# Attention with agents and a one-expert mixture on one core: a first batch's instructions reordered, constant products added, and the last blocks' scaling moved between engines

## The chip, the cores and the metric

The kernel runs on one core of one Trainium2 chip. The metric is the device time of one execution in microseconds (us); the median of several executions is compared. The core's engines are TensorE (PE in the rows; PEld is its weight loading), VectorE (DVE), ScalarE (ACT), GpSimd (POOL) and SyncE (SP), which here issues nearly all DMA transfers. Each engine works through its own list of instructions in order, and waits in that order.

## The reference

Four batches of 11456 tokens with 128 channels pass through an attention with 49 "agents" in the middle; the result is the input of a mixture of 8 experts with one expert per token.

```python
scale = 1.0 / np.sqrt(128)                       # sm(a, b): softmax over rows of scale * a @ b.T
agent_v = sm(agents, k) @ v                      # (49 x 128) per batch: needs all keys and values
attn    = sm(q, agents) @ agent_v                # per token
x       = attn.reshape(B * S, 128)               # 45824 tokens
logits  = x @ w_gate;  e = argmax(logits);  p = softmax(logits)[e]
out     = p * (relu(x @ w1[e]) @ w2[e])          # 128 -> 1024 -> 128
```

## The kernel before

**Per batch.** A batch's tokens come in 12 chunks (11 of 1024 tokens, one of 192). Keys: each chunk is loaded (`ld`), its sum of squares gives a power of two as scale (`scale_bits`, lines 232 and 236 on VectorE, 239 on GpSimd), it is split into two half-precision parts (`split`: L403, then L406, or L417 and L418), turned by a transposing DMA (`hT`, L432) and multiplied with the agents (`scores`, L475 to L479). After the last key the maximum is formed (`keymax`), the exponentials taken (`kexp`, L557 and L562), and the values multiplied (`values`: in the first batch L595, in later ones L612, which needs the parts `eh` that GpSimd's L574 and L582 help to make). `agentvalues` and `choose` then find the expert that most tokens of the batch want (`ei`, L826, named `gate["D"]`), and its weights are loaded (L264, L266) and folded with the agents' values into `Ah`, `Al` (L845 to L852). Queries give `E` (L722 to L730) and the matrix `M`, turned by another transposing DMA (L753).

**Steps.** The chosen expert is then applied to the whole batch in 184 steps (23 groups of 512 tokens by 8 slices of the hidden layer): L1341 and L1342 multiply `M` with `Ah`, `Al`; L1344 (ScalarE) and L1345 (VectorE) make `hh`; L1359 multiplies with `w2h`, `w2l`. 736 steps in all. The next batch's attention runs beside them. Its events stand in a list by step numbers: `KS1` are those of the second batch's keys, `QC`, `Q0` those of the first batch's queries from the fourth on, at step `Q0 + 13 * (c - 3)`. A scheduler then orders each engine's list; `queued("D")` keeps instructions behind `gate["D"]` on that instruction's engine, VectorE, alone.

**Before the steps.** The first batch has nothing to run beside, so TensorE waits for single results. `busy(n, x)` issues n products of constants (L526, 512 columns each) behind the instruction x, whose result nobody reads.

**Rank sums.** When a batch's routing is known, `leftover_ranks` sums where tokens of other experts go (L988 to L1005, on GpSimd in the first three batches).

**Tail.** Tokens that chose another expert than their batch's are gathered in 14 blocks of 128. Per block the expert's w1 and w2 are loaded and split (`weights_split`: L1198 on ScalarE, L1200 on VectorE, or instead of L1200 a second pass of ScalarE and GpSimd's L1203); `block_layer1` has 24 matmuls (L1212 to L1214), L1216 and L1217; `block_layer2` has 24 more (L1228 to L1230); `block_store` scales the result (L1237, VectorE) and scatters it (L1243, issued by GpSimd). The loop over u runs layer 1 of block u, then layer 2 of block u - 2, then the weights of block u + 5.

Of the kernel before, what the change touches and what calls it, by code (L numbers as in the profile page):

```python
# [16 lines left out]
AF = mybir.ActivationFunctionType  # L17
ALU = mybir.AluOpType
# [4 lines left out]
A = 49  # L23
# [22 lines left out]
KS0, KT0, KL0, VT0, VL0, QS0, QL0 = -200, 2, 4, 2, 1, (-175, -142, -141.5), (2.8, 1.2, 1.3)  # L46
VE, T1, TF0, TF1, TL, TLM, Q0 = 12, 1.75, 3, 1.5, 18, 10, 5

# [3 lines left out]
QM0, QG0 = (-145.5, -140, 0), ("K", "D", ("A", 1))  # L52
KS1 = [-142, -141.5] + [8.2 * i for i in range(10)]
KS2 = {0: 7, 1: 11}
# [17 lines left out]
FL, FLS, FW, FWJ, WA, FS, SPA, FSE = 148, (0, 2, 12), 104, 10.5, 7, 8, 7, 'D'  # L72
TSE, BL = 'D', 2
AHEAD, AHEAD0 = 3, 8
# [4 lines left out]
def agent_moe_kernel(ctx, tc, q, k, v, agents, wg, w1, w2, out):  # L79
    nc = tc.nc  # L80
# [141 lines left out]
    def queued(x):  # L222
        return tc.issue_after(gate[x].ins) if x in gate else nullcontext()
# [67 lines left out]
    def attention(b):  # L291
# [94 lines left out]

        def scaling(src, c, ss, p):
            SC[src, c] = scale_bits(ss, p, 1, "s" + src, AG["bits"] if src != "v" else None)

# [79 lines left out]
        def scores(src, c, ps):  # L469
            _, p, t = chunks[c]  # L470
            x = TT.pop((src, c))
            for i in range(t):
                o = ps[:p, i * A:(i + 1) * A]
                if how[src, c] == "X":
                    nc.tensor.matmul(o, x[:, i, :p], AG["T"], start=True, stop=True)  # L475
                    continue
# [52 lines left out]
        def keymax(i):  # L529
# [12 lines left out]
            else:  # L542
                pt = small_ps()
                x = nc.tensor.matmul(pt[:, :A], ones[:A, :], MX["d"][:A], start=True, stop=True)
                if first:
                    busy(6, x)
                mxb = MX["b"] = one.tile([P, A], F32, tag="mxb", name="mxb")
# [75 lines left out]
        def agentvalues(i):  # L623
# [12 lines left out]
            elif i == 2:  # L636
# [4 lines left out]
                if first:  # L641
                    pt = small_ps()
                    nc.tensor.matmul(pt[:, :A], AV["acc"][:, :D], both, start=True, stop=True)
                    AV["acc"] = pt[:, :A]
# [547 lines left out]
    def weights_split(u, j, eng):  # L1192
# [4 lines left out]
            [P, 2, FF], F16, tag=tag, name="wsp", **({} if tag == "ld" else dict(bufs=HLB if tag == "hl" else HTB[tag[2:]])))  # L1197
        nc.scalar.activation(hl[:, 0, :], x, AF.Copy, scale=m)  # L1198
        if eng == "D":
            nc.vector.scalar_tensor_tensor(hl[:, 1, :], x, m, hl[:, 0, :], op0=ALU.mult, op1=ALU.subtract)  # L1200
        else:
            nc.scalar.activation(x, x, AF.Copy, scale=m)
            nc.gpsimd.tensor_tensor(hl[:, 1, :], x, hl[:, 0, :], op=ALU.subtract)  # L1203
# [28 lines left out]
    def block_store(u):  # L1232
# [3 lines left out]
        yo = xg[1][:, u % 4, :]  # L1236
        nc.vector.tensor_scalar(yo, bh.pop(u)[:, :D], gt, None, op0=ALU.mult)  # L1237
        view = oviews[u]
# [286 lines left out]
```

## Time and profile before

| | us |
|---|---|
| median of 3 runs (lowest to highest) | 1103.39 (1100.06 to 1105.75) |
| the profiled execution, its own time | 1102.89 |
| its span, first to last instruction | 1101.2 |
| TensorE busy | 1021.1 (93%) |
| VectorE busy | 982.1 (89%) |
| ScalarE busy | 828.6 (75%) |
| GpSimd busy | 213.2 (19%) |

The profile is of one execution. The span leaves out 1.7 us that lie around it. A busy TensorE is not one at its peak, since it runs at one of two clocks, 1.2 or 2.4 GHz; the profile gives the granted clock as 0.5 or 1.0. Idle time counts only where the engine that waits is one that sets the pace.

### The profile page before, as it was taken

The page shows a single profiled execution, that of the slowest core. Times are in us where ns is not written, and L with a number is a line of the kernel's source. Part 1 is how long each engine was busy: PE and PEld are TensorE (multiplying, and loading weights), DVE is VectorE, ACT ScalarE, POOL GpSimd, SP SyncE. Part 2 cuts the span into 40 slices and gives each one's busy share as a digit, 9 for nine tenths or more (in the row PEclk, how much of TensorE's full clock was granted, in tenths as well). Part 3 has the DMA queues.
Part 4 walks back from the last instruction along what each step waited for, and adds up shares of the span by engine and source line. Part 5 has one row for each costly group of instructions (what it writes and reads, how often), then busy time and mean ns, then how long its engine had stood idle before and what let it go on. Part 6 is the DMA issues. An engine that isn't in the chain of part 4 may idle for free. (4 is left out here: it accounts for less than half of the span.)

```text
span 1101.2 us, 35748 instructions
## 1 busy us (share of the span) xinstructions
PE 1021.1 (93%) x14590; PEld 824.8 (75%) x14590; DVE 982.1 (89%) x2350; ACT 828.6 (75%) x1495; POOL 213.2 (19%) x373
## 2 busy tenths in 40 slices
PE   7979989999889999999999999999999999989995
PEld 7757767777667777777787777777777777767895
DVE  5659989998789999998999998998999999899894
ACT  6558767888678787889888887988677666667591
POOL 1020001233500011133400011232400223111043
PEclk9968999999899999999999999999999999999998
DMA  9779979544289899765399998563466556434460
GB/s 322 213 189 229 206 166 211 147 128 149 96 174 239 187 236 195 200 138 189 116 227 228 212 231 210 136 186 133 119 170 139 151 120 122 143 110 131 152 216 15
DMA packets 269384, 189.44 MB, mean 172 GB/s; under 512 B 211273, under 2 KB 235426, under 8 KB 269216
## 3 DMA queue, kind: packets, MB, share of 16 engines
q1 hardware_dynamic: 267648, 184.87, 66.6%
q0 software_dynamic: 1568, 2.25, 1.1%
q8 instruction: 115, 1.88, 0.7%
q14 instruction: 53, 0.43, 0.1%
HBM read 99.75 MB, written 36.43 MB: 124 GB/s over the span
## 5 line engine op out<-in xcount | busy, mean ns | idle before, releaser
L1359 PEld LDWEIGHTS <-hh 128*128 128x128 f16 x8640 | 547.6, 99 | 170.2 <-issue 7.4
L1359 PE MATMUL py<-w2h,hh 128*128 128x128 f16 (+1 forms) x5760 | 606.5, 220 | 2.7 <-ACT hh L1344 1.4
L1359 PE MATMUL py<-w2l,hh 128*128 128x128 f16 (+1 forms) x2880 | 523.8, 220 | 1.7 <-DVE w2l L899 1.7
L1344 ACT ACTIVATE hh<-ph 128x512 f16<-128x512 f32 (+1 forms) x736 | 412.9, 583 | 133.4 <-PE ph L1342 125.4
L1345 DVE SCALAR_TENSOR_TENSOR hh<-ph,hh 128x512 f16<-128x512 f32 (+1 forms) x736 | 476.8, 666 | 31.9 <-ACT hh L1344 30.6
L1341 PE MATMUL ph<-M,Ah 128*128 128x512 f16 (+1 forms) x736 | 276.1, 376 | 22.5 <-DVE hh L1345 21.4
L1342 PE MATMUL ph<-M,Al 128*128 128x512 f16 (+1 forms) x736 | 276.2, 375 | 0.0
L406 DVE SCALAR_TENSOR_TENSOR hl<-ld,mul,hl 128x1024 f16<-128x1024 f32 (+1 forms) x115 | 139.9, 1220 | 18.3 <-ACT hl L403 16.9
L403 ACT ACTIVATE hl<-ld,mul 128x1024 f16<-128x1024 f32 (+1 forms) x117 | 127.0, 1092 | 24.2 <-DVE mul L236 23.5
L369 ACT ACTIVATE jk<-ld 128x1024 f16<-128x1024 f32 (+1 forms) x124 | 124.3, 1003 | 10.5 <-DMA ld<-in_k_dram 10.3
L239 POOL TENSOR_SCALAR div<-hb,bits 128x1 int32<-128x1 int32 (+1 forms) x88 | 28.6, 325 | 430.2 <-DVE hb L232 407.5
L1342 PEld LDWEIGHTS <-Al 128*128 128x128 f16 x736 | 72.1, 98 | 31.2 <-issue 29.1
L1341 PEld LDWEIGHTS <-Ah 128*128 128x128 f16 x736 | 73.5, 100 | 4.8 <-issue 3.1
L1372 DVE TENSOR_TENSOR yo<-py,cs 128x512 f32<-128x512 f32 (+1 forms) x92 | 61.4, 668 | 1.0 <-PE py L1359 0.9
L477 PE MATMUL ps_s<-agh,hT 128*128 128x49 f16 x580 | 52.9, 185 | 3.6 <-DMA hT<-hl 2.1
L479 PE MATMUL ps_s<-agh,hT 128*128 128x49 f16 x580 | 52.8, 184 | 0.0
L478 PE MATMUL ps_s<-agl,hT 128*128 128x49 f16 x580 | 52.7, 184 | 0.0
L574 POOL TENSOR_TENSOR es<-es,S 128x392 f32<-128x392 f32 (+1 forms) x33 | 32.1, 973 | 102.7 <-ACT S L562 96.4
L477 PEld LDWEIGHTS <-hT 128*128 128x128 f16 x606 | 49.5, 97 | 3.2 <-DMA hT<-hl 3.2
L478 PEld LDWEIGHTS <-hT 128*128 128x128 f16 x606 | 48.3, 97 | 2.3 <-issue 2.0
L479 PEld LDWEIGHTS <-hT 128*128 128x128 f16 x606 | 48.2, 97 | 0.1
L562 ACT ACTIVATE S<-S,ln 128x392 f32<-128x392 f32 (+1 forms) x48 | 27.7, 598 | 17.4 <-DVE S L557 17.3
(323 smaller groups left out, 1349.1 us busy)
## 6 DMA issues: line engine op xcount, KB each, us to landing
ld<-in_k_dram SPq DMA_DIRECT2D x44, 512.0 KB
ld<-in_v_dram SPq DMA_DIRECT2D x44, 512.0 KB
ld<-in_q_dram SPq DMA_DIRECT2D x44, 512.0 KB
out_dram<-yo SPq DMA_DIRECT2D x88, 256.0 KB
w1e<-in_moe_w_dram SPq DMA_DIRECT2D x18, 512.0 KB
w2e<-in_moe_w_dram SPq DMA_DIRECT2D x18, 512.0 KB
exps<-E SPq DMA_DIRECT2D x44, 196.0 KB
wn<-in_moe_w_dram SPq DMA_DIRECT2D x16, 512.0 KB
```

The costliest lines, as they stand in the source:

```text
L369: nc.scalar.activation(jk[:p, :t * D], x[:p, :t, :].rearrange("p t d -> p (t d)"), AF.Square, accum_out=ss[:p])
L403: nc.scalar.activation(hi[:p, :t, :], x[:p, :t, :], AF.Copy, scale=m)
L406: nc.vector.scalar_tensor_tensor(lo[:p, :t, :], x[:p, :t, :], m, hi[:p, :t, :], op0=ALU.mult, op1=ALU.subtract)
L477: nc.tensor.matmul(o, x[:, 0, i, :p], AG["h"], start=True, stop=False)
L478: nc.tensor.matmul(o, x[:, 0, i, :p], AG["l"], start=False, stop=False)
L479: nc.tensor.matmul(o, x[:, 1, i, :p], AG["h"], start=False, stop=True)
L1341: x1 = nc.tensor.matmul(ph[:, :nn], st['Ah'][:, f, :], m, start=True, stop=False)
L1342: nc.tensor.matmul(ph[:, :nn], st['Al'][:, f, :], m, start=False, stop=True)
L1344: x2 = nc.scalar.activation(hh[:, 0, :nn], ph[:, :nn], AF.Relu)
L1345: x3 = nc.vector.scalar_tensor_tensor(hh[:, 1, :nn], ph[:, :nn], 0.0, hh[:, 0, :nn], op0=ALU.max, op1=ALU.subtract)
L1359: mm_ = lambda l, r, **k: nc.tensor.matmul(o, l, r, skip_group_check=True, **k)
L1372: nc.vector.tensor_tensor(yo[:p, :n, :], py[:p, :n * D].rearrange("p (i d) -> p i d", d=D), cs.unsqueeze(2).broadcast_to([p, n, D]), op=AL ...
```

## The change

Six edits:

1. The scale bits of the second batch's first two keys (`KS2` holds chunks 0 and 1) are made under `queued("D")`: VectorE's L232 and L236 for them stand behind the expert's choice. Their events move from step -142 and -141.5 to -141.9 and -141.4.
2. Constant products: four after the scores of the first batch's first query chunk, four after the product of `agentvalues(2)` in the first batch, and four in place of six after `keymax(2)`.
3. `Q0` goes from 5 to 1: every event of the first batch's queries from the fourth chunk on is four steps earlier, loads, transposes and `M` too.
4. `TSE` goes from `'D'` to `'DDDP'`: of the 14 splits of the tail's loop, those of w2 for three blocks (8, 10 and 12) go by ScalarE and GpSimd.
5. That path is rewritten: GpSimd scales the weights in place, ScalarE rounds, GpSimd subtracts.
6. `block_store` scales on ScalarE.

```diff
-VE, T1, TF0, TF1, TL, TLM, Q0 = 12, 1.75, 3, 1.5, 18, 10, 5
+VE, T1, TF0, TF1, TL, TLM, Q0 = 12, 1.75, 3, 1.5, 18, 10, 1
-KS1 = [-142, -141.5] + [8.2 * i for i in range(10)]
+KS1 = [-141.9, -141.4] + [8.2 * i for i in range(10)]
-TSE, BL = 'D', 2
+TSE, BL = 'DDDP', 2
         def scaling(src, c, ss, p):
+            with queued("D") if b == 1 and src == "k" and c in KS2 else nullcontext():
+                scaling1(src, c, ss, p)
+
+        def scaling1(src, c, ss, p):
             SC[src, c] = scale_bits(ss, p, 1, "s" + src, AG["bits"] if src != "v" else None)
-                    nc.tensor.matmul(o, x[:, i, :p], AG["T"], start=True, stop=True)
+                    m = nc.tensor.matmul(o, x[:, i, :p], AG["T"], start=True, stop=True)
+                    if (src, c, i) == ("q", 0, t - 1):
+                        busy(4, m)
-                    busy(6, x)
+                    busy(4, x)
-                    nc.tensor.matmul(pt[:, :A], AV["acc"][:, :D], both, start=True, stop=True)
+                    busy(4, nc.tensor.matmul(pt[:, :A], AV["acc"][:, :D], both, start=True, stop=True))
-        nc.scalar.activation(hl[:, 0, :], x, AF.Copy, scale=m)
         if eng == "D":
+            nc.scalar.activation(hl[:, 0, :], x, AF.Copy, scale=m)
             nc.vector.scalar_tensor_tensor(hl[:, 1, :], x, m, hl[:, 0, :], op0=ALU.mult, op1=ALU.subtract)
         else:
-            nc.scalar.activation(x, x, AF.Copy, scale=m)
+            nc.gpsimd.tensor_scalar(x, x, m, None, op0=ALU.mult)
+            nc.scalar.copy(hl[:, 0, :], x)
             nc.gpsimd.tensor_tensor(hl[:, 1, :], x, hl[:, 0, :], op=ALU.subtract)
-        nc.vector.tensor_scalar(yo, bh.pop(u)[:, :D], gt, None, op0=ALU.mult)
+        nc.scalar.activation(yo, bh.pop(u)[:, :D], AF.Copy, scale=gt)
```

The lists of the changed kernel have other line numbers: from 6 to 7 more than before in the parts shown here.

**First place.** VectorE, at the end of the first batch's values. `acc` are the values' sums, `av` the agents' values, `ei` the expert; `hb` and `mul` are the scale bits of the second batch's first two keys. Before:

```order
L746 TENSOR_TENSOR mm_143<-E,mm_143 128x8x49
L232 TENSOR_SCALAR hb<-ss 128x1
L236 TENSOR_SCALAR mul<-hb 128x1
L599 COPY acc<-pv 49x129
L600 COPY acc<-pv 49x129
L634 TENSOR_SCALAR rs<-ps_small 128x49
L635 RECIPROCAL rs<-rs 128x49
L232 TENSOR_SCALAR hb<-ss 128x1
L645 TENSOR_TENSOR av<-ps_small,rs 128x2x49
L236 TENSOR_SCALAR mul<-hb 128x1
```

After:

```order
L752 TENSOR_TENSOR mm_143<-E,mm_143 128x8x49
L605 COPY acc<-pv 49x129
L606 COPY acc<-pv 49x129
L640 TENSOR_SCALAR rs<-ps_small 128x49
L641 RECIPROCAL rs<-rs 128x49
L651 TENSOR_TENSOR av<-ps_small,rs 128x2x49
```

Both pairs of L232 and L236 have moved; they now stand behind `ei`, eleven and thirteen rows further down than the last row shown.

**Second place.** GpSimd, near the end of the first batch's steps, where the rank sums (`C`, `cp`) meet the second batch's values (`es`, `eh`). Before, from the subtraction of the tenth value chunk on:

```order
L582 TENSOR_TENSOR eh<-S,eh 128x392
L239 TENSOR_SCALAR div<-hb 128x1
L988 TENSOR_TENSOR C<-oh,npri 128x8x90
L994 TENSOR_TENSOR C<-C 128x8x11
L996 TENSOR_TENSOR C<-C 128x8
L994 TENSOR_TENSOR C<-C 128x8x11 x6
L1001 TENSOR_TENSOR cp<-cp,C 128x8 x2
L990 COPY C<-gs 128x8x90
L1001 TENSOR_TENSOR cp<-cp,C 128x8 x5
L574 TENSOR_TENSOR es<-es,S 128x392
L1001 TENSOR_TENSOR cp<-cp,C 128x8 x5
L1003 TENSOR_TENSOR C<-C,cp 128x8x88
```

After, from the subtraction of the ninth on:

```order
L588 TENSOR_TENSOR eh<-S,eh 128x392
L994 TENSOR_TENSOR C<-oh,npri 128x8x90
L1000 TENSOR_TENSOR C<-C 128x8x11
L1002 TENSOR_TENSOR C<-C 128x8
L1000 TENSOR_TENSOR C<-C 128x8x11 x3
L996 COPY C<-gs 128x8x90
L580 TENSOR_TENSOR es<-es,S 128x392
L1000 TENSOR_TENSOR C<-C 128x8x11 x3
L588 TENSOR_TENSOR eh<-S,eh 128x392
L1007 TENSOR_TENSOR cp<-cp,C 128x8 x5
L239 TENSOR_SCALAR div<-hb 128x1
L1007 TENSOR_TENSOR cp<-cp,C 128x8 x7
```

The rank sums begin one value chunk earlier and hold the tenth chunk's two instructions between them; the eleventh's come after all of them.

**Third place.** VectorE in the tail, from the first block's `hh` on. `wsp` are the split weights (L1200 before, L1206 after), `yb` the scaled results. Before:

```order
L1217 SCALAR_TENSOR_TENSOR hh<-ph,hh 128x512 x4
L1237 TENSOR_SCALAR yb<-pyb,fgt 128x128
L1200 SCALAR_TENSOR_TENSOR wsp<-w2e,tsm_18231,wsp 128x1024
L1200 SCALAR_TENSOR_TENSOR wsp<-w1e,tsm_18227,wsp 128x1024
L1217 SCALAR_TENSOR_TENSOR hh<-ph,hh 128x512 x2
L1237 TENSOR_SCALAR yb<-pyb,fgt 128x128
L1200 SCALAR_TENSOR_TENSOR wsp<-w1e,tsm_18227,wsp 128x1024
L1200 SCALAR_TENSOR_TENSOR wsp<-w2e,tsm_18231,wsp 128x1024
```

After:

```order
L1224 SCALAR_TENSOR_TENSOR hh<-ph,hh 128x512 x4
L1206 SCALAR_TENSOR_TENSOR wsp<-w2e,tsm_18239,wsp 128x1024
L1224 SCALAR_TENSOR_TENSOR hh<-ph,hh 128x512
L1206 SCALAR_TENSOR_TENSOR wsp<-w1e,tsm_18235,wsp 128x1024
L1224 SCALAR_TENSOR_TENSOR hh<-ph,hh 128x512
L1206 SCALAR_TENSOR_TENSOR wsp<-w1e,tsm_18235,wsp 128x1024
L1224 SCALAR_TENSOR_TENSOR hh<-ph,hh 128x512
L1206 SCALAR_TENSOR_TENSOR wsp<-w2e,tsm_18239,wsp 128x1024
```

The scaling of results is gone from this list, a subtraction of w2 in three of seven blocks is gone too, and `hh` stands between the splits that are left.

## Rows read from the trace of the kernel before

**Rows 1.** Busy time by stretch: stretch, length, then busy us (instructions) of PE, PEld, DVE, ACT, POOL; granted clock; DMA share; GB/s.

```profile
57.85:74.92 17.07, 15.29 (x70) 13.23 (x69) 7.62 (x31) 7.28 (x11) 4.53 (x3) 0.50 0.84 192
...
153.43:156.84 3.41, 3.41 (x40) 2.57 (x36) 3.06 (x8) 1.20 (x3) 0.00 (x0) 0.50 1.04 144
...
289.96:296.79 6.83, 5.99 (x53) 4.38 (x53) 2.18 (x4) 2.23 (x4) 1.89 (x5) 0.50 0.25 100
```

**Rows 2.** Timeline of PE, 40 to 78: start, length, instruction [idle before <- ended by].

```profile
41.73 2.67 PE L526 MATMUL ps_w<-ones 128*128 128x512 bf16 x6
...
44.64 10.13 PE L595 MATMUL pv<-ld,S 128*49 128x129 f32 x180
57.43 0.42 PE L630 MATMUL ps_small<-both,acc 128*128 128x49 f32 x2 [2.66 <-DVE acc L600]
...
59.95 0.60 PE L817 MATMUL ps_small<-wg_sb,avs 128*128 128x8 f32 x2 [1.78 <-DVE avs L651]
...
72.30 3.26 PE L845 MATMUL pa<-w1e,av 128*128 128x512 f32 x4
...
77.67 0.82 PE L1341 MATMUL ph<-M,Ah 128*128 128x512 f16 x3 [0.25 <-ACT Ah L851]
```

**Rows 3.** Timeline of DVE, 56 to 70.

```profile
56.51 0.15 DVE L232 TENSOR_SCALAR hb<-ss 128x1 int32<-128x1 int32 x1 [6.06 <-ACT jk L369]
...
59.17 0.15 DVE L232 TENSOR_SCALAR hb<-ss 128x1 int32<-128x1 int32 x1 [0.57 <-ACT jk L369]
...
69.91 1.21 DVE L864 TENSOR_REDUCE am<-w1e 128x1 f32<-128x1024 f32 x1
```

**Rows 4.** Timeline of ACT and of SP's queue, 63 to 68.

```profile
67.25 0.59 ACT L462 COPY xF<-pxT 128x512 f32<-128x512 f32 x1 [0.27 <-PE pxT L456]
...
63.62 0.37 SPq L264 DMA_DIRECT2D w1e<-in_moe_w_dram  x1
```

**Rows 5.** Who PE waited for, 77 to 324: us in total, times, longest.

```profile
PE ps_s L612 <- POOL eh L582: 4.0, 1, 4.0
PE ps_s L762 <- DMA M<-mm: 3.3, 1, 3.3
...
PE ps_s L477 <- DMA hT<-hl: 1.8, 1, 1.8
```

**Rows 6.** Timeline of SP's queue, 142 to 151.

```profile
142.98 5.10 SPq L432 DMA_TRANSPOSE hT<-hl  x2
...
148.80 1.29 SPq L753 DMA_TRANSPOSE M<-mm  x1
```

**Rows 7.** Timeline of POOL, 277 to 291.

```profile
277.09 2.78 POOL L988 TENSOR_TENSOR C<-oh,npri 128x720 f32<-128x720 f32 x1 [2.34 <-DVE rs L802]
...
289.83 0.92 POOL L582 TENSOR_TENSOR eh<-S,eh 128x392 f16<-128x392 f32 x1
```

**Rows 8.** Groups from 1044 to the end: operation xcount | busy us, mean ns | idle before.

```profile
L1212 PE MATMUL ph<-xs,wsp 128*128 128x128 f16 x112 | 21.9, 225 | 2.5 <-DVE hh L1217 2.5
...
L1216 ACT ACTIVATE hh<-ph 128x512 f16<-128x512 f32 x28 | 16.4, 592 | 12.6 <-PE ph L1214 12.4
...
L1200 DVE SCALAR_TENSOR_TENSOR wsp<-w2e,tsm,wsp 128x1024 f16<-128x1024 f32 x7 | 9.0, 1280 | 0.0
...
L1237 DVE TENSOR_SCALAR yb<-pyb,fgt 128x128 f32<-128x128 f32 x14 | 4.8, 345 | 1.4 <-PE pyb L1230 1.4
...
L1181 ACT ACTIVATE xs<-fxT,mul 128x128 f16<-128x128 f32 x2 | 0.7, 388 | 0.0
```

**Rows 9.** Timelines of DVE and of POOL around 180.

```profile
179.96 1.28 DVE L406 SCALAR_TENSOR_TENSOR hl<-ld,mul,hl 128x1024 f16<-128x1024 f32 x1
...
180.03 1.99 POOL L746 TENSOR_TENSOR mm<-E,mm 128x392 f16<-128x392 f32 x1 [1.86 <-ACT hl L403]
```

**Rows 10.** Groups of POOL by form, whole span.

```profile
L418 POOL TENSOR_TENSOR hl<-ld,hl 128x1024 f16<-128x1024 f32 x2 | 4.2, 2124 | 3.4 <-ACT ld L417 3.4
...
L990 POOL COPY C<-gs 128x720 f32<-128x720 f32 x3 | 2.4, 789 | 0.0
```

## The prediction, made before the changed kernel was run

> **What bounds the kernel now.** I read the page's busy shares and slices first: PE is busy for 93% of the span, so it sets the pace, and a gain is either a wait of PE or a stretch at the lower clock. The page's chain of waits tells only of the last microsecond and is no help. Busy time by stretch with the granted clock shows three places at 0.5, which is 1.2 GHz, on which edits bear: 17.07 us in the first batch's choice and weights, with PE busy for 15.29 of it, then 3.41 us and 6.83 us in the steps [rows 1]. PE's timeline shows what stands in the first: waits of 2.66 and 1.78 us, both for VectorE [rows 2]. VectorE's own timeline shows why: its L232 waited 6.06 us and again 0.57 us for a ScalarE pass over a key, and the copies of `acc` stand behind it [rows 3]. The list of who PE waited for gives two large waits in the first batch's steps, 4.0 us for `eh` and 3.3 us for `M` [rows 5]; the two later low stretches follow these. In the tail the reader is to see that PE waited 2.5 us for VectorE's `hh`, and ScalarE was idle for 12.6 us [rows 8].
>
> **Part 1, to the first step (edits 1 and 2): -6 us, from -9 to -3.4.** Two products fewer behind `keymax(2)`: one takes 2.67 / 6 = 0.45 us [rows 2], so -0.9. The values L595 ended at 44.64 + 10.13 = 54.77 and L630 began at 57.43 [rows 2]; behind L595 stood the wait of L232 until 56.51, then L236 and the copies [rows 3]. With L232 out of the way the copies run at once, and what is left of the 2.66 is their own time, about 0.75: -1.9. The second L232 had VectorE idle for 0.57 [rows 3], inside the 1.78 us wait for `avs`: -0.57. So L817 comes 3.4 us earlier. The four new products behind `agentvalues(2)` are 4 x 0.45 = 1.8 us at the lower clock. They lie in that wait, which is now about 1.2: at the lower clock they overrun it by 0.6, which I leave in the range; at the upper one they cost nothing.
>
> From L817 (59.95) to the first step's L1341 (77.67) 17.7 us passed [rows 2]. The lower bound on the gain is that nothing changes here: PE is busy nearly throughout, so at 1.2 GHz the 3.4 us are all. But the clock fell at 57.85, in the wait that is now filled, just after the one that is now short [rows 1, 2]. If it stays up, PE's work there, 15.29 us, would halve, and something else is last: w1e. SP issued it at 63.62, 3.67 after L817, and VectorE's L864, which reads it, ran at 69.91 [rows 3, 4], so it was there after at most 6.3 us. Now issue is at 56.55 + 3.67 = 60.2 and landing at 66.5 or before. From L845 to L1341 it was 77.67 - 72.30 = 5.4 us [rows 2], of which L845's own 3.26 would fall by half. In the new orders of VectorE and PE, L864 and L845 stand ahead of the third query chunk's last pieces, half a chunk of scores, which now come before L1341 instead: 1.75 us (half of the 16 matmuls of that kind) at the lower clock. First step: between 66.5 - 1 + 5.4 - 1.6 + 0.9 = 70 and 66.5 + 5.4 + 1.75 = 73.7. I take the middle, 71.7, for -6; -9 needs w1e a little over 1 us before that bound.
>
> Cover of edit 1: the keys whose bits are later have their ScalarE and GpSimd passes from about 59 instead of 57. The ScalarE passes now mix with the copies of query chunks `xF`, the last of which stood at 67.25 [rows 4]; it may come as late as before while PE is faster. Their scores stand at the eighth step, ten microseconds beyond the first: nothing. In SP's list the next loads of keys and queries now stand ahead of the first `M`, not behind it: nothing for the steps.
>
> **Part 2, queries four steps sooner (edit 3): `M`, -3 us, from -5 to 0.** A step takes about (1044 - 77.67) / 736 = 1.3 us. PE waited 3.3 us for the sixth query chunk's `M` [rows 5] and then had 3.41 us at the lower clock with PE busy throughout [rows 1], worth up to 1.7. SP ran two transposes `hT` in 5.10 us from 142.98, and only at 148.80 that `M` [rows 6]. By the lists of before, its transpose stood 3.5 steps ahead of the logits that read it; now 6.8, that is 3.3 steps or 4.3 us more, over the 3.3 waited. All of it would be -5. But the transposes of queries and keys now fall elsewhere against each other, and L477's wait of 1.8 us for an `hT` [rows 5] is what one collision costs. 5 - 1.8 is about 3.
>
> **Part 3, rank sums (edit 3 again): -4 us, from -7.4 to 0.** GpSimd began them with L988 at 277.09, for 2.78 us, and the tenth value chunk's subtraction L582 came only at 289.83 [rows 7]. PE waited 4.0 for it [rows 5], and 6.83 us at the lower clock followed [rows 1], worth up to 3.4. With the last queries four steps, 5.3 us, sooner, the sums start sooner, and that subtraction stands in their midst; the eleventh is behind all of them, a chunk later (some 5 steps, 7 us). By the events' steps it is then ready one step before its use. So near, a third wait is as likely as none: I take about half of 7.4.
>
> **Part 4, the tail (edits 4 to 6): -2.5 us, from -4.9 to +4.1.** VectorE loses 14 x 0.345 = 4.8 us of scaling and three of seven subtractions, 3 x 1.28 = 3.8 us [rows 8], of its work where it was the latest: PE's wait for it was 2.5 [rows 8]. ScalarE takes 14 scalings; the nearest row is L1181, a scaled copy at 0.388 [rows 8], 5.4 us, against 12.6 idle. GpSimd takes three scalings, between L990's copy of 128x720, 0.79, or 1.12 at 1024 columns, and L418's 2.12, and three subtractions at L418's 2.12 [rows 10]: 3 x (3.24 to 4.25) = 9.7 to 12.7 us, where it has little else but to issue gathers and scatters. A block's weights are asked for five blocks ahead, at about 2.8 us of PE a block, so the path's length of some 6 us is covered if GpSimd isn't held.
>
> It can be held. At 180 VectorE's L406 ran from 179.96 to 181.24 and GpSimd's L746, begun at 180.03, took 1.99 instead of the 0.92 that the same form takes in L582 [rows 7, 9]: it ended 0.78 after L406, as if its own work had been barred until then. The same would work the other way against VectorE's splits. If all 12.7 us excluded VectorE, 12.7 - 8.6 = +4.1; if none, the 2.5 and as much again in the weights' lead, to -4.9. I take -2.5, the wait seen, since only part of these passes can meet a split.
>
> This is the page "SBUF — State Buffer" of the Trainium skill, section "Who interferes with whom": a VectorE instruction with two inputs from SBUF and a GpSimd instruction that reads SBUF share a port pair, and the later one waits for the whole of the other. The trace agrees (1.99 against 0.92). By that rule alone Part 4 is +4.1 and the time about 6.6 us later than I forecast.
>
> **Sum.** -6 - 3 - 4 - 2.5 = -15.5 on the profiled execution's own 1102.89, which is 0.5 below the median of 1103.39. So 1087.4 for it, and 1087.5 as rounded for the median, the difference being within the runs' spread. The terms' ends do not all fall together: adding their distances from the middle as independent ones (2.6 and 3, 3 and 2, 4 and 3.4, 6.6 and 2.4) gives +8.6 and -5.5, so 1082 to 1096 for this case alone.
>
> **Rivals.**
> - *Earlier, but given back in the first batch (17%), 1097.* The steps start 6 us sooner, but the second batch's keys and values are not sooner: their loads and transposes run on SP's queue, and PE's waits for them (1.8, 3.3 and 4.0 [rows 5]) move or grow. Then only the ramp counts: 1103.4 - 6 = 1097. For it: the waits are for DMA and GpSimd, not for PE. Against: PE is busy in nearly all of the rest.
> - *GpSimd's passes bar VectorE in the tail (13%).* The worked +4.1 of Part 4 instead of -2.5: 1087.5 + 6.6 = 1094. For it: the L746 row. Against: only three blocks of 14 take the path.
> - *The clock stays up and each wait goes (10%).* Every term at its far end, -9 - 5 - 7.4 - 2.5 = -24: 1079.5.
> - *Slower: transposes collide (5%).* Queries four steps sooner meet the keys' transposes on SP's queue. If a query's transposes, a key's and an `M` together outlast the lead of 6.8 steps, 8.9 us (two `hT` took 5.10 and `M` 1.29 [rows 6], so it takes three and a half `hT` in a row to decide it), each such meeting costs 3.3 and half of 3.41, 5.0 us; with 4 of the 9 later chunks so, +20, against the -6 and -2.5: 1103.4 + 20 - 8.5 = 1115.
> - *The products don't do what they are put there for.* The clock still falls: Part 1 is -3.4, the time 1090. This lies inside the forecast's range and has no chance of its own.
>
> **How the numbers follow.** The forecast has 55%, the rivals 17, 13, 10 and 5. The predicted time is the forecast's, 1087.5. From 1078 to 1099 leaves out the slower rival and the tails of the others, not over 2 in 10. Half a per cent, 5.5 us, is about what a measurement can tell from no change here: faster means below 1097.9. That is the forecast, nearly all of the barred tail and the high-clock case, and somewhat over half of the given-back one: 0.84. The rest of that one and a corner of the forecast are the same, 0.11; slower is the collision, 0.05.
>
> **What would show it.** Right in Part 1: L630 within a microsecond of L595's end, L817 near 56.5, L1341 near 72, and 1.0 as the granted clock for most of 58 to 72. Part 2: no wait of PE for `M` above 1 us and no low stretch at 150. Part 3: none for `eh` in the first batch, nor at 290. Part 4: no wait for VectorE's `hh`, splits on VectorE still at 1.28. Wrong: a first step at 74 or later; a new wait for an `hT` or an `eh` above 3 us, with a low stretch behind it; splits well above 1.28 beside GpSimd's passes.

## The result, and the profile after

| | before | changed |
|---|---|---|
| median, same chip (lowest to highest, 6 runs each) | 1100.39 (1096.77 to 1105.75) | 1087.36 (1080.15 to 1093.36) |
| the profiled execution, its own time | 1102.89 | 1085.47 |
| its span | 1101.2 | 1083.8 |

The ratio of the two is 0.9879, with a 95% interval from 0.9842 to 0.9916: 13 us less, clear of the spread. A second set of runs on another chip gave 1096.00 against 1111.20, 0.9862 (0.9819 to 0.9904). Chips differ by more than the edits here, so kernels are compared by their ratio to the kernel before on their own chip.

Where the time went is read best from one line: the 736 starts of the matmul L1348 (L1341 before), one for each step. Taken from PE's timelines, start by start, the changed kernel's lead over the profile before is 7.9 us at the first step, 6.3 at the 49th, 10.3 at the 145th, 15.6 at the 185th (the second batch's first) and 15.4 at the last; the span ends 17.4 earlier. So in these two traces the gains lie in four places and nowhere else: 6.3 up to and just behind the first step, 4.0 around the sixth query chunk, 5.3 around the rank sums, 2.0 in the tail. The three later batches change next to nothing (0.2 lost).

PE's timeline after, beside [rows 2] (start, length, instruction, idle before and what ended it):

```profile
43.14 10.13 PE L601 MATMUL pv<-ld,S 128*49 128x129 f32 x180 [0.33 <-issue]
53.93 0.42 PE L636 MATMUL ps_small<-both,acc 128*128 128x49 f32 x2 [0.65 <-DVE acc L606]
...
55.89 0.39 PE L823 MATMUL ps_small<-wg_sb,avs 128*128 128x8 f32 x2 [0.46 <-DVE avs L657]
...
62.50 3.64 PE L851 MATMUL pa<-w1e,av 128*128 128x512 f32 x4
...
69.76 0.81 PE L1348 MATMUL ph<-M,Ah 128*128 128x512 f16 x3
```

The wait for `acc` is 0.65 instead of 2.66, that for `avs` 0.46 instead of 1.78, and the first step stands at 69.76 instead of 77.67. The stretches (length, busy PE, PEld, DVE, ACT, POOL, granted clock), beside [rows 1]:

```profile
53.27:62.45 9.18, 6.82 (x49) 5.35 (x48) 4.54 (x27) 6.10 (x10) 2.18 (x3) 1.00 0.95 263
62.45:65.86 3.41, 3.36 (x4) 1.51 (x5) 3.38 (x3) 1.80 (x3) 2.50 (x2) 0.50 1.03 311
```

The clock stayed at 2.4 GHz from the values' end to 62.45 and was at 1.2 GHz for 3.41 us only, under L851, against 17.07 before. Who PE waited for in the first batch's steps, beside [rows 5]:

```profile
PE ps_s L618 <- POOL eh L588: 2.6, 2, 1.6
PE ps_s L483 <- DMA hT<-hl: 2.6, 3, 1.3
PE ps_small L878 <- DVE am L871: 2.5, 1, 2.5
```

The 3.3 for `M` is gone; the 4.0 for `eh` has become 1.6 and 1.0. There is no low stretch at 150 or at 290 any more; one of 3.41 us stands at 308, behind the 2.5 for `am`. SP's queue and GpSimd's timeline show why, beside [rows 6] and [rows 7]:

```profile
131.29 1.76 SPq L436 DMA_TRANSPOSE hT<-hl  x1
...
134.82 1.99 SPq L759 DMA_TRANSPOSE M<-mm  x1
136.92 2.69 SPq L436 DMA_TRANSPOSE hT<-hl  x1
```

```profile
261.43 1.78 POOL L994 TENSOR_TENSOR C<-oh,npri 128x720 f32<-128x720 f32 x1 [3.36 <-DVE rs L808]
...
269.75 0.92 POOL L588 TENSOR_TENSOR eh<-S,eh 128x392 f16<-128x392 f32 x1
...
277.01 0.92 POOL L588 TENSOR_TENSOR eh<-S,eh 128x392 f16<-128x392 f32 x1
```

`M` now stands between the two `hT`, and the rank sums begin 15.7 us sooner, of which 10 are the lead that the steps already had there. In the tail (groups from the last L1348 to the end, operation, count, busy, mean ns, idle), beside [rows 8] and [rows 10]:

```profile
L1219 PE MATMUL ph<-xs,wsp 128*128 128x128 f16 x112 | 21.8, 225 | 1.0 <-DVE hh L1224 0.8
...
L1206 DVE SCALAR_TENSOR_TENSOR wsp<-w1e,tsm,wsp 128x1024 f16<-128x1024 f32 x7 | 10.9, 1563 | 0.7 <-ACT wsp L1205 0.7
L1208 POOL TENSOR_SCALAR w2e<-w2e,tsm 128x1024 f32<-128x1024 f32 x3 | 10.3, 3432 | 19.2 <-DMA w2e<-in_moe_w_dram 18.9 <-SPq L1495 0.3
...
L1210 POOL TENSOR_TENSOR wsp<-w2e,wsp 128x1024 f16<-128x1024 f32 x3 | 7.3, 2427 | 0.0
L1244 ACT ACTIVATE yb<-pyb,fgt 128x128 f32<-128x128 f32 x14 | 5.1, 367 | 2.3 <-PE pyb L1237 1.9
```

PE waits 0.8 us for `hh` instead of 2.5. But VectorE's w1 splits take 1563 ns in the mean and not 1280, and GpSimd spends 17.6 us on its six passes.

### The profile page after: what moved, and what is told of

Its sections match the earlier page's. It is cut to its first block, busy times and chain, and to the rows that moved or that the text cites. A ratio compares the mean times of both kernels' runs of the same rounds, so it can differ in the third digit from the quotient of the medians.

```text
span 1083.8 us, 35771 instructions
## 1 busy us (share of the span) xinstructions
PE 1012.6 (93%) x14596; PEld 817.6 (75%) x14596; DVE 979.7 (90%) x2333; ACT 833.1 (77%) x1509; POOL 227.7 (21%) x379
## 5 line engine op out<-in xcount | busy, mean ns | idle before, releaser
L1348 PE MATMUL ph<-M,Ah 128*128 128x512 f16 (+1 forms) x736 | 274.7, 374 | 24.3 <-DVE hh L1352 23.0
L410 DVE SCALAR_TENSOR_TENSOR hl<-ld,mul,hl 128x1024 f16<-128x1024 f32 (+1 forms) x115 | 139.2, 1215 | 17.2 <-ACT hl L407 15.5
L1348 PEld LDWEIGHTS <-Ah 128*128 128x128 f16 x736 | 73.2, 100 | 3.9 <-issue 2.8
L483 PE MATMUL ps_s<-agh,hT 128*128 128x49 f16 x564 | 51.7, 185 | 4.2 <-DMA hT<-hl 2.6
L485 PE MATMUL ps_s<-agh,hT 128*128 128x49 f16 x564 | 51.5, 185 | 0.0
```

The lines of the kernel that those rows point to most:

```text
L410: nc.vector.scalar_tensor_tensor(lo[:p, :t, :], x[:p, :t, :], m, hi[:p, :t, :], op0=ALU.mult, op1=ALU.subtract)
L483: nc.tensor.matmul(o, x[:, 0, i, :p], AG["h"], start=True, stop=False)
L485: nc.tensor.matmul(o, x[:, 1, i, :p], AG["h"], start=False, stop=True)
L1348: x1 = nc.tensor.matmul(ph[:, :nn], st['Ah'][:, f, :], m, start=True, stop=False)
```

## Experiments

All line numbers are the changed kernel's. "Lead" is how much sooner than in the profile before the n-th L1348 starts (from the timelines, as above); a minus sign means sooner.

| kernel | ratio to before (95%) | step 1 | 49 | 145 | 185 | tail, us |
|---|---|---|---|---|---|---|
| changed, first trace | 0.9879 (0.9842 to 0.9916) | -7.9 | -6.3 | -10.3 | -15.6 | 57.3 |
| changed, second trace | 0.9862 (0.9819 to 0.9904) | -7.2 | -6.1 | -10.1 | -15.1 | 58.9 |
| scale bits early | 0.9930 (0.9904 to 0.9956) | -2.1 | -1.5 | -5.5 | -11.4 | 57.2 |
| no products at av | 0.9884 (0.9822 to 0.9945) | -12.6 | -11.3 | -15.4 | -20.5 | 57.4 |
| Q0 = 5 | 0.9950 (0.9919 to 0.9981) | -3.4 | -2.9 | -4.6 | -5.4 | 56.6 |
| only chunks 3 to 7 sooner | 0.9938 (0.9907 to 0.9969) | -7.4 | -5.4 | -9.8 | -10.5 | 56.4 |
| Q0 = -1 | 0.9948 (0.9927 to 0.9970) | -5.5 | +0.4 | +0.3 | -6.3 | 60.7 |
| batch 2's weights | 0.9883 (0.9853 to 0.9913) | -7.6 | -5.9 | -9.9 | -15.8 | 59.2 |

"Tail" is from the last L1348 to the span's end; it was 59.3 before. The rows with a tail under 58 come from chips on which the kernel before took 1099 to 1100, the other three from two on which it took 1111 and 1114: there the steps from 608 to 680 take 8 to 11 us more in each of these traces, which is no part of what is compared. Each lead also holds when the first batch's values began. That was at 43.14 us in the first trace and from 40.00 to 44.26 in the others, although the lists up to there are the same in all of them. So up to 4 us of a difference between two rows can come from ahead of the edits that are compared; what is gained between two steps of one row is free of that.

**Edit 1 undone.**

```diff
-            with queued("D") if b == 1 and src == "k" and c in KS2 else nullcontext():
+            with nullcontext():
-KS1 = [-141.9, -141.4] + [8.2 * i for i in range(10)]
+KS1 = [-142, -141.5] + [8.2 * i for i in range(10)]
```

> The changed kernel with edit 1 undone: the scale bits of the second batch's first two keys are again made ahead of the expert choice. Theory as predicted (edit 1 alone carries 1.9 + 0.57 us and keeps the clock up): the product behind the copies of acc (L636, line numbers of the changed kernel) starts about 2.5 us after the values end instead of 0.65, the clock falls at about 57 and the first step comes at 73 to 75 instead of 69.8. Rival (the key loads landed 2.7 us earlier in the changed kernel, so the ScalarE passes over the keys end at 53.84 and 55.17 and the scale bits hardly wait): L636 starts about 0.8 us later, the agents' values less than 1 us later, and the first step at 70 to 71.5. In both the time after step 160 keeps whatever the first step lost; nothing changes in the tail.

Measured, in PE's and ACT's timelines of this kernel:

```profile
55.94 0.42 PE L636 MATMUL ps_small<-both,acc 128*128 128x49 f32 x2 [1.73 <-DVE acc L606]
...
58.46 0.39 PE L823 MATMUL ps_small<-wg_sb,avs 128*128 128x8 f32 x2 [1.01 <-DVE avs L657]
```

```profile
53.85 1.06 ACT L369 ACTIVATE jk<-ld 128x1024 f16<-128x1024 f32 x1 [3.73 <-DMA ld<-in_k_dram]
```

Between the two expectations. The waits come back, smaller than before: from the values' end to L823 it took 4.24 us, against 2.62 with the change and 5.18 before. The difference to before is the key's load: ScalarE's pass over it began 0.37 us before the values' end here and 0.57 after it in the profile before. So the edit itself is worth 1.6 us up to L823, not 2.5. Behind it the clock was at 0.5 from 59.14 to 72.79 and the first step came at 75.57; how much of that part is the edit's is open, since kernels with one and the same code up to there differ by 5 us, as shown below.

**The four products behind `agentvalues(2)` left out.**

```diff
-                    busy(4, nc.tensor.matmul(pt[:, :A], AV["acc"][:, :D], both, start=True, stop=True))
+                    nc.tensor.matmul(pt[:, :A], AV["acc"][:, :D], both, start=True, stop=True)
```

> The changed kernel without the four constant products behind agentvalues(2); the products of the other two places stay. Theory (they are there for the clock): TensorE is idle for about 1.2 us before L823, the granted clock falls to 0.5 at about 56 and stays there for most of the choice, and the first step comes 2.5 to 5 us later, at 72 to 75. Rival (the short wait alone doesn't matter, the clock stays up until about 62 as it did): the first step within 0.4 us of 69.8.

The theory failed and the rival did not quite hold. L823 came 2.62 us after the values' end, to the hundredth as with the products; the clock did fall early, at 53.87, and was up again at 57.28:

```profile
53.87:57.28 3.41, 3.41 (x17) 2.91 (x16) 1.53 (x14) 1.87 (x3) 0.53 (x2) 0.50 1.00 130
57.28:65.10 7.82, 7.47 (x55) 5.54 (x55) 4.56 (x13) 6.82 (x10) 4.26 (x2) 1.00 1.05 282
```

The values themselves began at 40.0 here and not at 43.1, since the clock was up sooner (the sixteen products L479 from 9.86 on took 1.99 us, and 3.61 in the changed kernel), so the leads of this row are 3 us too good. The first step stood 14.97 us behind the values' end, sooner than in any kernel with the products. The times, 0.9884, tell no difference. The early fall is not the missing products' doing alone: the kernel with the results on VectorE, below, has all four, and its clock fell at 53.48, also for 3.41 us. What these four products bring can't be shown here, and one trace doesn't show that they do harm. The other two places of edit 2 were not tried by themselves.

**Edit 3 undone, whole and in part.**

```diff
-VE, T1, TF0, TF1, TL, TLM, Q0 = 12, 1.75, 3, 1.5, 18, 10, 1
+VE, T1, TF0, TF1, TL, TLM, Q0 = 12, 1.75, 3, 1.5, 18, 10, 5
```

```diff
-                t = (Q0 + QC * (c - 3) if first and c > 2 else ...
+                t = (Q0 + 4 * (c > 7) + QC * (c - 3) if first and c > 2 else ...
```

> The changed kernel with Q0 back at 5. Theory (both gains inside the first batch's steps come from the four steps): TensorE waits again for the sixth query chunk's M, 3 us or more, and for the tenth value chunk's eh, about 4 us, each followed by a stretch at 0.5; the lead over the kernel before is about 6 us at step 48 and still 5 to 7 us at step 184, against 15.6 with the change; the time is 8 to 10 us above the changed kernel's. Rival (the earlier first step by itself moved loads and transposes so that these waits went): the lead grows to over 12 us without the four steps.

> The changed kernel with the four earlier steps kept for the query chunks 3 to 7 and taken back for chunks 8 to 11. Theory (the M gain hangs on the sixth chunk alone, the eh gain on when the last queries' routing lets GpSimd begin the rank sums): the wait for M stays away and the lead at step 144 is about 10 us as with the change; the rank sums begin about 5 us later, TensorE waits for eh about 4 us with a low stretch behind it, and the lead at step 184 is about 10 to 11 instead of 15.6. Rival (the eh gain comes from the first step being earlier or from other traffic): the lead at step 184 is 15 to 16 as with the change.

Who PE waited for from the first step to 324, with Q0 at 5:

```profile
PE ps_s L618 <- POOL eh L588: 5.0, 1, 5.0
PE ps_s L768 <- DMA M<-mm: 3.2, 1, 3.2
```

and with the later chunks alone put back:

```profile
PE ps_s L618 <- POOL eh L588: 4.0, 1, 4.0
```

Both theories hold in the main. With Q0 at 5 both waits are back and end at 148.95 and 286.24, and the lead grows by 2.5 us between steps 49 and 185, where it grows by 9.3 with the change. With only the chunks 3 to 7 sooner, `M` costs nothing (4.3 us gained by step 145) and the rank sums cost what they did: the lead at 185 is 10.5, 5.1 short of 15.6. So the two terms are separate, and each is in the place that the prediction gave it.

One thing came out otherwise. With Q0 at 5 no low stretch followed the wait for `M`, against the expectation, and the lead grew by 1.7 us up to step 145 although that wait was there: just what half of the stretch of 3.41 at 153 [rows 1] had cost the kernel before. From there to step 185 it grew by another 0.8. So of the 4.0 and 5.3 us, 2.3 and 4.5 hang on the four steps by this trace; the rest is a difference between executions, most of it in the clock.

**The same code once more.**

> The changed kernel as it is, for a second trace. Theory (the first step's time hangs on how the granted clock falls in this execution, since the kernel with Q0 at 5 has the same code up to there and took its first step at 74.3 with the clock at 0.5 from 61.9 to 75.5): the first step lies anywhere from 69 to 75, with L636 within 0.7 us of the values' end and L823 1.9 us behind it whatever the clock does; the lead gained between steps 48 and 184 stays within 1 us of the 9.3 of the first trace. Rival (the first trace is typical, the clock is up through the choice): the first step at 69 to 71 again.

The first step was at 70.49, so this trace alone would speak for the rival. But eleven traces have the same instructions on TensorE, VectorE, ScalarE and GpSimd from the values' end to the first step, and there they differ. That way took 16.5 and 17.7 us in the changed kernel, 16.6 to 16.8 in four others, 17.7 with Q0 at -1 (whose lists differ only further on), and 19.6 to 21.6 in the last four, among them 20.5 with Q0 at 5, whose stretch (columns as above) reads

```profile
61.87:75.52 13.65, 13.65 (x49) 8.66 (x50) 6.10 (x11) 6.96 (x11) 3.70 (x2) 0.50 0.82 232
```

In all of them the clock fell between 2.2 us before L851's start and 1.0 us behind it, and came back after 3.4 to 13.7 us, in which PE was busy for 84 to 100%. The longer it was down, the longer the way: 16.5 to 16.8 us with 3.4 at 0.5, 17.7 with 6.8, 19.6 with 10.2, 20.5 to 21.6 with 13.7 (the 21.6 with another 3.4 at 53.48). Whether that is long or short is not the edits' doing, and it is worth up to 5 us. It may be a good part of the spread of the 6 runs, 13.2 us, of which only one has a trace. The gain from step 49 to 185 was 9.0 and so within 1 us of the first trace.

**The tail's edits.** First all splits of the loop on VectorE again, then the results on VectorE again, then more splits for GpSimd:

```diff
-TSE, BL = 'DDDP', 2
+TSE, BL = 'D', 2
```

```diff
-        nc.scalar.activation(yo, bh.pop(u)[:, :D], AF.Copy, scale=gt)
+        nc.vector.tensor_scalar(yo, bh.pop(u)[:, :D], gt, None, op0=ALU.mult)
```

```diff
-TSE, BL = 'DDDP', 2
+TSE, BL = 'DP', 2
```

> The changed kernel with TSE back at 'D': all 14 splits of the tail's loop on ScalarE and VectorE, results still scaled on ScalarE. From the last L1348 to the end it was 59.3 us in the kernel before and 57.2 with the change. Theory (VectorE is the tail's late engine, and taking 3.8 us of subtractions from it is worth about half of the gain): 58 to 59, and TensorE waits 1 to 2.5 us for hh. Rival (GpSimd's passes bar VectorE's splits for as long as they relieve it, 2.56 and 1.97 us instead of 1.28 for two splits in the trace): 56.5 to 57.5, no longer than with the change.

> The changed kernel with the results scaled on VectorE again, the three w2 splits still on ScalarE and GpSimd. Theory (14 x 0.345 = 4.8 us back on the late engine): from the last L1348 to the end 58 to 59.3 instead of 57.2, TensorE waits over 1.5 us for hh. Rival (VectorE has slack once the three subtractions are gone): 57 to 57.5.

> The changed kernel with TSE at 'DP': 7 of the 14 splits of the loop (all of w2) on ScalarE and GpSimd instead of 3. A GpSimd scaling took 3.43 and a subtraction 2.43 us in the changed kernel, 41 us for seven of both, where the stretch has about 45. Theory (GpSimd's passes are too dear, and each bars VectorE's splits): from the last L1348 to the end 60 to 70 us instead of 57.2, with TensorE waiting for wsp or hh, and VectorE's splits well above 1.28 us on the mean. Rival (GpSimd has the time, and VectorE gains 5 us more): 55 to 57.

On one chip, with the changed kernel's second trace beside them at 58.9 and a ratio of 0.9862: all on VectorE, 59.5 and 0.9896 (0.9860 to 0.9933); results on VectorE, 68.5 and 0.9976 (0.9945 to 1.0007); seven splits for GpSimd, 68.9 and 0.9975 (0.9947 to 1.0003). The first is 0.6 us longer than with the change and PE waits 0.6 us for `hh`, less than the theory's 1 to 2.5; its tail also had 3.41 us at 0.5 from 1050.84, which the change's had not. Taken alone, the three splits on GpSimd are worth little, as the rival has it. The second is 9 us beyond what either expected: moving 4.8 us of scalings back costs 9.6 us. In the third PE waited not for `wsp` or `hh` but once, for 5.2 us, for ScalarE's `jk` (sums of squares of gathered tokens), and 3.41 and 6.83 us of its tail were at 0.5. VectorE's and GpSimd's timelines of the second:

```profile
1056.59 3.77 DVE L1206 SCALAR_TENSOR_TENSOR wsp<-w2e,tsm,wsp 128x1024 f16<-128x1024 f32 x1
...
1062.94 2.90 DVE L1206 SCALAR_TENSOR_TENSOR wsp<-w1e,tsm,wsp 128x1024 f16<-128x1024 f32 x1
...
1072.10 3.33 DVE L1188 SCALAR_TENSOR_TENSOR xs<-fxT,mul,xs 128x128 f16<-128x128 f32 x2
```

```profile
1057.11 2.16 POOL L1210 TENSOR_TENSOR wsp<-w2e,wsp 128x1024 f16<-128x1024 f32 x1
...
1062.63 2.12 POOL L1210 TENSOR_TENSOR wsp<-w2e,wsp 128x1024 f16<-128x1024 f32 x1 [1.41 <-ACT wsp L1209]
...
1073.13 2.14 POOL L1210 TENSOR_TENSOR wsp<-w2e,wsp 128x1024 f16<-128x1024 f32 x1
```

All three of GpSimd's subtractions met work of VectorE's with two inputs. The two splits ended 1.09 us after the subtraction that they met (1060.36 against 1059.27, 1065.84 against 1064.75), as if they had begun only at its end; undisturbed they take 1.28. The two L1188 take 0.60 in the kernel with seven splits on GpSimd. So VectorE lost 2.5, 1.6 and 2.7 us. What PE waited for shows how that reached the time:

```profile
PE ph L1219 <- DVE hh L1224: 4.0, 1, 4.0
PE ps_small L1179 <- ACT jk L1176: 3.6, 1, 3.6
```

ScalarE's copy ahead of `jk` had waited 1.99 us, up to the end of the split of 3.77, and the `hh` stood behind the two L1188 and one more split. Behind each of these waits, which ended at 1062.90 and 1077.28, lay 3.41 us at 0.5, from 1063.82 and from 1077.47. So the 9.6 us are waits of PE and a lower clock behind them, and not VectorE's lost time by itself. In the changed kernel two splits were held up by a subtraction, the last two rows of each timeline:

```profile
1041.89 1.28 DVE L1206 SCALAR_TENSOR_TENSOR wsp<-w2e,tsm,wsp 128x1024 f16<-128x1024 f32 x1 [0.23 <-ACT wsp L1205]
...
1045.97 2.56 DVE L1206 SCALAR_TENSOR_TENSOR wsp<-w1e,tsm,wsp 128x1024 f16<-128x1024 f32 x1
...
1055.72 1.97 DVE L1206 SCALAR_TENSOR_TENSOR wsp<-w1e,tsm,wsp 128x1024 f16<-128x1024 f32 x1
```

```profile
1040.24 3.53 POOL L1208 TENSOR_SCALAR w2e<-w2e,tsm 128x1024 f32<-128x1024 f32 x1 [2.03 <-DMA w2e<-in_moe_w_dram]
...
1045.02 2.44 POOL L1210 TENSOR_TENSOR wsp<-w2e,wsp 128x1024 f16<-128x1024 f32 x1
...
1054.10 2.51 POOL L1210 TENSOR_TENSOR wsp<-w2e,wsp 128x1024 f16<-128x1024 f32 x1
```

and ended 1.07 and 1.08 us after GpSimd: 1.28 + 0.69 lost. The split in the first row lay in a scaling of GpSimd's and lost nothing. Five kernels whose tail is the change's (scale bits early, Q0 = 5, only chunks 3 to 7 sooner, Q0 = -1, batch 2's weights) even show a split of 3.41 to 3.79 each. In the three of them on chips like the first trace's the tail was still 56.4 to 57.2, as with the change. So a split at that price was borne where the scalings were on ScalarE; the 9.6 us came where VectorE had 4.8 us more to do. With seven splits on GpSimd, VectorE's w1 splits took 2846 ns in the mean.

**Edit 5 undone.**

```diff
-            nc.gpsimd.tensor_scalar(x, x, m, None, op0=ALU.mult)
-            nc.scalar.copy(hl[:, 0, :], x)
+            nc.scalar.activation(hl[:, 0, :], x, AF.Copy, scale=m)
+            nc.scalar.activation(x, x, AF.Copy, scale=m)
```

> The changed kernel with edit 5 undone: in the three w2 splits that are not VectorE's, ScalarE rounds the scaled weights and scales them in place, as before, and GpSimd only subtracts. GpSimd's passes in the tail fall from 17.6 to about 7.3 us, ScalarE's grow by about 3.7. Theory (it is the subtractions, with two inputs, that bar VectorE, and GpSimd's scalings matter little): one or two of VectorE's splits still take over 1.5 us, the tail from the last L1348 to the end stays within 1 us of the changed kernel's 56.4 to 58.9. Rival (the scalings are what costs): no split of VectorE's above 1.5 us and the tail at 55 to 56.

The theory's first half held, its second didn't, and the rival is out: one split, met by a subtraction, took 1.52 and the others 1.27 to 1.29, but the tail was 62.6, against 59.2 of the kernel with the second batch's weights on the same chip, and the ratio 0.9906 (0.9872 to 0.9941). Two stretches at 0.5, 3.4 us each, lay in this tail and not in the other. ScalarE was late too: VectorE waited 9.7 us for its `hh` and not 3.7. What of the 3.4 us is the edit's and what the clock's is open.

**The whole tail as before.**

```diff
-TSE, BL = 'DDDP', 2
+TSE, BL = 'D', 2
-        nc.scalar.activation(yo, bh.pop(u)[:, :D], AF.Copy, scale=gt)
+        nc.vector.tensor_scalar(yo, bh.pop(u)[:, :D], gt, None, op0=ALU.mult)
```

> The changed kernel with the whole tail as before (edits 4 to 6 undone): 14 splits and 14 scalings on VectorE. On the chips of the other tail kernels the tail, from the last L1348 to the end, took 58.9 with the change, 59.5 with all splits on VectorE and results on ScalarE, 68.5 the other way round. Theory (the tail's edits are worth 1 to 2.5 us, the rest of the gain lies before the steps' end): the tail at 59.5 to 61.5, TensorE waiting 2 to 3 us for hh, and a ratio to the kernel before between 0.988 and 0.991, against 0.986 to 0.988 for the whole change. Rival (the tail's edits carry nothing): the tail at 58.5 to 59.4, ratio as for the whole change.

```profile
PE ph L1219 <- DVE hh L1224: 2.5, 3, 0.9
```

The wait for `hh` is back at 2.5, as before; the tail took 59.5, the kernel 0.9887 (0.9860 to 0.9914). On chips like this one five traces with the change's tail gave 56.4 to 57.4, so by the traces the three edits are worth 2.1 to 3.1 us together; the times alone can't tell 2 us. The tail lies just at the theory's lower end, the ratio within it. If the 0.6 of the splits, taken on another chip, holds here too, most of it is the scalings' move to ScalarE; that is argued from two chips and not shown.

**Two steps further.**

```diff
-VE, T1, TF0, TF1, TL, TLM, Q0 = 12, 1.75, 3, 1.5, 18, 10, 1
+VE, T1, TF0, TF1, TL, TLM, Q0 = 12, 1.75, 3, 1.5, 18, 10, -1
```

> The changed kernel with Q0 at -1, two steps further. Theory (the rank sums would then end before the tenth and eleventh value chunk are due, whose eh TensorE still waited for by 1.6 and 1.0 us): those two waits go, the lead at step 184 is 17 to 18.5 us over that at the first step's level of the same trace plus what the first step gained. Rival (transposes collide: a query's, a key's and an M within the same steps): a wait for hT or M above 2 us comes up in the first 150 steps, and the lead gained from step 48 to 184 is below the 9.3 of the changed kernel.

Both happened. There is no wait for `eh` left, but

```profile
PE ph L1348 <- DVE hh L1352: 8.8, 7, 3.6
...
PE ps_s L483 <- DMA hT<-hl: 2.7, 2, 2.2
```

the steps now wait for VectorE, once for 3.6 us, and a key's transpose comes 2.2 us late, with low stretches at 107 and 270. From the first step to the 49th 5.9 us are lost (1.6 with the change), and from there to 185 only 6.7 gained, less than 9.3. The rival decides it; of the three values 5, 1 and -1, 1 is the best.

**The wait that was left.** In the second batch's weights TensorE still waited 2.5 us for L871:

```diff
-                nc.vector.tensor_tensor(am[:, 1:2], am[:, 0:1], AV["avm"], op=ALU.mult)
+                (nc.gpsimd if b == 1 else nc.vector).tensor_tensor(am[:, 1:2], am[:, 0:1], AV["avm"], op=ALU.mult)
-            at(base + tw + w0 + (i * w1_ if first else WO[i]), weights, i)
+            at(base + tw + w0 + (i * w1_ if first else WO[i] + (2.4 if b == 1 and i == 1 else 0)), weights, i)
```

> The changed kernel with one wait more taken away, that of the second batch's weights: there the product of am with avm (L871) runs on GpSimd instead of VectorE, and the event that sums it and squares w2e comes 2.4 steps later. In the changed kernel L871 stood behind an L410 that waited for ScalarE, which waited for w2e, and TensorE waited 2.5 us for it at 305 and then had 3.4 us at 0.5. Theory (that wait is the whole of it): no wait for L878 above 0.5 us, no low stretch at 308, and the lead over the kernel before grows by 3.5 to 4.5 us between steps 160 and 200, where the changed kernel gained 0.2; the time is 4 us below the changed kernel's. Rival (the weights are late anyway, by w2e or by L851): the wait turns up at L851 or at the first steps of the second batch, and the lead grows by less than 1 us.

The wait went, and the lead was 19.4 us at step 177, 3.8 more than with the change. Eight steps on it was 15.8 again:

```profile
307.51 0.33 PE L878 MATMUL ps_small<-am,ones 128*128 128x1 f32 x2
...
316.77 0.18 PE L483 MATMUL ps_s<-agh,hT 128*128 128x49 f16 x1 [1.25 <-DVE mul L236]
...
322.03 0.39 PE L1348 MATMUL ph<-M,Ah 128*128 128x512 f16 x1 [2.28 <-DVE mul L236]
```

PE waited 1.25 and 2.28 us at the change of batches, with a low stretch from 322.67: the rival, at a place one line on from those it named. VectorE, further ahead in its list, had waited 1.52 us for ScalarE's `hh` there, and ScalarE 1.51 and 0.51 us for loads of a key and a query chunk. No version better than the change came out of this.

## Why the prediction was right, step by step

**The whole.** 1087.5 was predicted, 1087.36 measured; the match to a tenth is luck, the range is not. -15.5 was forecast from 1102.89. In the profiles the terms add to -17.4, and the medians fell by 13.0, since that of before moved down by 3 us with more runs: misses on either side, which cancelled.

**Part 1: -6 predicted, -6.3 measured at the 49th step (-7.9 at the first).** The steps to L823 came as said: 4.06 us sooner, 3.4 forecast. The values' start was 1.5 sooner and not 0.9, because the low stretch at 40.8, in which the six products lay, is not there. No trace with edit 2 has it, but what keeps it away was not tried, and the values began anywhere from 40.0 to 44.4 in those traces, at 40.0 in the three in which the clock was up from 10 us on. The size given to edit 1 was too large by the luck of a load: 1.6 us by its own experiment, 2.47 in the sum. The overrun feared from the four products did not come. w1e was issued 2.7 us after L823 and L870 waited for it until 62.48: 3.9 us after issue, well inside the bound of 6.3 that the sum used. The clock did not simply stay up, nor did it fall where it had fallen; it fell later, under L851, which took 3.64 instead of the 1.6 counted on. L851 began 4 us before the bound of 66.5 for w1e, and the first step came 7.3 us behind it and not 4.7 to 7.2: that the first step still lies within 2 us of the forecast is two misses against each other.

**Part 2: -3 predicted, -4.0 measured.** The mechanism was shown by both experiments on Q0, for 2.3 of the 4.0; the other 1.7 is a low stretch that the kernel with Q0 at 5 didn't have either, so it was no sure follower of the wait, as the sum had it. Of the 1.8 us kept back for a new collision, part was spent: PE now waits 1.0 and 1.3 us for an `hT`, where it had waited 1.8 once.

**Part 3: -4 predicted, -5.3 measured.** Shown by the kernel with the later chunks put back; 0.8 of it came with Q0 at 5 too. "A third wait is as likely as none" came out as two short ones, 1.6 and 1.0, with no low stretch behind them; that the clock would stay up was worth more than the half allowed.

**Part 4: -2.5 predicted, -2.0 by the trace, -2.2 by its undoing.** One term was mis-sized: GpSimd's scaling of 128x1024 was put between 1.12 and 2.12 us and took 3.43 in the mean, 2.87 where nothing met it, so its passes came to 17.6 us and not to 9.7 to 12.7. The copy and the subtraction that bounded it were the wrong neighbours. One sign of being wrong came: splits well above 1.28, at 2.56 and 1.97. That the price stayed small is only in part due to the reason given ("only part of these passes can meet a split"; two of three subtractions cost a split time). The larger part is edit 6: with the scalings still on VectorE, all three subtractions met its work and the tail lost 9.6 us, while with them on ScalarE even a split of 3.79 cost nothing.

**The rivals.** "Given back in the first batch" did not happen in the change, but its mechanism is real: 1.6 us between the first step and the 49th, and 3.5 us in the last experiment. Port exclusion was rightly a case of its own. In the change it cost VectorE 2 us and PE nothing that shows; the worked +4.1 adds up passes and leaves out what a late pass holds up, which made the tail 9.6 us longer than the change's in the kernel one edit away. The page "SBUF — State Buffer" of the Trainium skill, section "Who interferes with whom", states that the loser waits for the whole instruction. The ends 1.07 to 1.09 us behind GpSimd's subtractions agree. Beside its scalings L1208, which read one tensor, they don't: a split that lay in one took its 1.28 in the changed kernel, and in other kernels the splits that one held up took 1.32 to 3.05 us and ended some 0.66 before it did, not behind it. Here the measurement decides. Collisions on SP's queue stayed below 1.4 us at Q0 = 1 and reached 2.2 at -1.

## What to carry to other kernels

Price each wait together with the clock behind it, and give the clock's share as a range from zero: the same instructions had it low for 3.4 to 13.7 us, and the same wait for `M` had 3.41 us at 0.5 behind it in one kernel and none in another. Before giving GpSimd a pass with two inputs from on-chip memory, look at which two-input passes of VectorE can meet it, and at whether VectorE has the slack to lose a whole pass there: with slack 3.79 us for a split cost nothing, without it three meetings cost 9.6. A wait that goes is worth what the next event in line allows; follow the lead step by step beyond the place, since nearly all of 3.8 us here was gone eight steps later.

## What the hardware showed that was not expected

The exclusion also struck at an unlooked-for place, a product of one column in the ramp. VectorE's and GpSimd's timelines of the changed kernel:

```profile
62.48 1.22 DVE L870 TENSOR_REDUCE am<-w1e 128x1 f32<-128x1024 f32 x1 [2.67 <-DMA w1e<-in_moe_w_dram]
...
64.09 1.90 DVE L871 TENSOR_TENSOR am<-am,avm 128x1 f32<-128x1 f32 x1
```

```profile
63.85 2.12 POOL L422 TENSOR_TENSOR hl<-ld,hl 128x1024 f16<-128x1024 f32 x1 [0.91 <-ACT ld L421]
```

L871 takes 0.15 us in the three later batches; here it ended at 65.99, with GpSimd's subtraction (65.97). In the second trace of the change and with Q0 at 5 it took 1.34 and 1.36 at this place. It cost nothing here, since PE was still at L851 and the scores behind it until 66.8.

Which of the two waits doesn't follow from the recorded starts alone. In six kernels a split that is recorded as begun 0.14 to 0.53 us before a subtraction ended 1.09 us behind it, as the one at 1056.59 above. Splits begun 0.67 to 1.01 us before one took their 1.28, and the subtraction took 2.28 to 2.63 instead of 2.12 to 2.17. What decides it in between is open.

On two chips the kernel before took 1111.20 and 1114.05, against 1099.28 to 1101.44 elsewhere, and the changed kernel 1096.00 against 1087.36. In the seven traces from these chips the steps from 608 to 680 take 6.5 to 11.1 us more than in the profile before; PE stands idle for 9.4 to 12.4 us in them, against 4.6 to 5.6 in the other traces, and six of the seven have a stretch or two at 0.5 there. Why it waits more is open.
